# Attention of the next batch element in six large blocks instead of twelve, beside a Strassen-like channel mixing on one core

## The chip, the cores and the metric

The kernel runs on one NeuronCore of a Trainium2 chip. The metric is the device time of one execution in microseconds. The core has five engines that work side by side and wait for one another through semaphores: TensorE (PE, with its weight loads shown apart as PEld), VectorE (DVE), ScalarE (ACT), GpSimd (POOL) and SyncE (SP), which here only issues DMA transfers.

## The reference

Everything is float32: 8 batch elements, 12 heads, sequence 448, head size 64, so 768 channels.

```python
# attention, per element and head
q_n, k_n = rmsnorm(q, g_q), rmsnorm(k, g_k)
attn = softmax(q_n @ k_n.T / sqrt(64))
x = attn @ v                      # heads side by side: (448, 768) per element

# mixer, per element
h  = relu(x.T @ w_tok1) @ w_tok2  # token mixing, 448 -> 256 -> 448
u  = x + h.T
h2 = relu(u @ w_ch1) @ w_ch2      # channel mixing, 768 -> 1536 -> 768
out = u + h2
```

The mixer of an element needs the whole attention of that element, and nothing of any other element.

## The kernel before

**What runs when.** `whole` writes one long program. Its loop over `b` emits the mixing of element `b`, and, spread into it, the attention of element `b + 1` (`AHEAD = 1`). The last element's mixing (`b = 7`) therefore stands alone. In what follows "phase b" is one round of this loop. A phase is, on TensorE: `tok1` (L685) and `tok2` (L693) for the token mixing; then the channel mixing as block-wise products after Strassen and Winograd: `ch1` (L809) makes 21 products (3 column groups `mp` of 7 products `i`), `ch2` with group 0 (L866) makes 14 halves (7 products, `j` = 0 and 1, which share one PSUM tile), and `ch2` with group 1 makes 7 more at the end. Each of these 42 items is 6 matmuls of 128x128 weights with 224 columns; the trace shows every float32 matmul as two records. Element 0 is mixed with plain products (L781) while its weights are converted from 64-bit floats. This conversion (`convert_first`, L264 to L282) uses two small tiles from `cv_pool`.

**Product results.** Every `ch1` product goes to a PSUM tile `m_ps` from a pool of two (`ps_M`), and must be read out before the second product after it can start. By `i`, the reader is: 0 ScalarE (L818), 1, 2, 3 VectorE (L814), 4 ScalarE (L830, followed by two GpSimd additions), 5 and 6 VectorE. `put_off` keeps some work until the beginning of the next product, such as the two VectorE maxima L839 after product 5. `ch2` is alike (L875, L879).

**Attention.** Heads are handled in pairs, and pairs two at a time: `t` counts the pairs of pairs, three to an element. For each `t` there are seven key blocks `k`. `score(t, k)` is four 64x64 matmuls (L385), one in each quarter of TensorE, into two PSUM tiles of the pool `ps_S` (four tiles), then two exponentials on ScalarE (L389) into a tile `e`, of which there are four. `values` (L459) multiplies the exponentials with `v`. `group_sums` (L427) adds up the seven `e` tiles, the first two additions on GpSimd and the rest on VectorE; `row_sums` (L439) finishes the sum on TensorE; `denominators` (L488 to L505) inverts and scales on VectorE. `score`, `values` for one `k`, and `row_sums` are of the same size on TensorE; they are called units of attention here, 45 in a full phase.

**Preparing q and k** for the next `t`: `square` (ScalarE, L1173), `reduce` (VectorE, L1187), `roots`, which is `fold` (four ScalarE copies, L1195), `guess` (VectorE, L1204 and L1209) and three `newton` steps (nine small VectorE operations, L1228 to L1230); then `scale` (L350) and `turn_qk` (VectorE transposes L365, one ScalarE multiplication L368). `square` writes one shared tile `sq`, so the second pair's square waits for the first pair's reduce.

**The order.** On the four compute engines the order is the order in which the program is written (`manual_schedule`); each engine works its list strictly in turn. SP's list is ordered by the framework. `att_step(g)` makes the items of a quarter of one `t`: `tiled`, a block of 3 or 4 units of attention on TensorE, and around it the items for the other engines. There are 12 such steps in a phase. `merge` interleaves lists of items (cost, function) in proportion to their costs, so that the 12 steps are spread evenly over `tok1` with `h = 1`, `tok2`, `ch1` and most of `ch2`. The last 4 halves of `ch2` group 0 and group 1 (`last`) have no attention beside them.

**DMA.** Weights come back from a scratch area in units (L740), eight buffers ahead; `load_units` for a product waits until the buffer of an earlier product is free. Loads of q and k (L1154, 16 for each `t`), of `v` (L338), the attention result's way through DRAM (`send_x`, L639, and `load_x`, L646), and the output (L629) share the same SP queue.

Of the kernel before, what the change touches and what calls it, by code (L numbers as in the profile page):

```python
# [8 lines left out]
F32 = mybir.dt.float32  # L9
U32 = mybir.dt.uint32  # L10
# [34 lines left out]
def whole(ctx, tc, shifted, pre, q, k, v, g_q, g_k, moe_w_tok1, moe_w_tok2, moe_w_ch1, moe_w_ch2, out):  # L45


    nc = tc.nc
# [3 lines left out]
    B, H, S, D = q.shape  # L52
# [3 lines left out]
    P = 128  # L56
    NS = 4
    R = S // NS
    NPAIR = H // 2
    NP = B * NPAIR  # L60
# [5 lines left out]
    HS = S // 2  # L66
    KC, KF = NC // 2, NF // 2
# [3 lines left out]
    NK = S // D  # L71
    NB = S // 32
    assert S == NK * D and NPAIR % 2 == 0 and D % 32 == 0

    UNITS = 8

    pool = lambda name, bufs, **kw: ctx.enter_context(tc.tile_pool(name=name, bufs=bufs, **kw))
    const = pool("const", 1)
    raw_pool = pool("raw_pool", 5)
    cv_pool = pool("cv_pool", 2)  # L80
    pre.st_pool = pool("st_pool", 2)
    pre.nt_pool = pool("nt_pool", 2)
    qkT_pool = pool("qkT_pool", 3)
# [17 lines left out]
    w1_sb = const.tile([P, NS, DT], F32, name="w1_sb")  # L101
    w2_sb = const.tile([P, NJ, NS, R], F32, name="w2_sb")
    hb = pre.hb

    ws1 = dram.tile([KF // 2, NQ, P, KC, 2, P], F32, name="ws1")
    ws2 = dram.tile([2, NQ, P, 3, 2, P], F32, name="ws2")
# [2 lines left out]
    st = dict(pre.st)  # L109
# [18 lines left out]
                pending.pop(0)[1]()  # L128

    WCOLS = 512

    def weight_chunks():

# [121 lines left out]
    def convert_first(i):  # L257

        if chunks[i][1][0].dtype != I64:
            return  # L260
        rows, n = chunks[i][0], columns(i)
        lo, hi = (st["raw", i][0:rows, 0:n, w] for w in range(2))
        e = cv_pool.tile([P, WCOLS], U32, name="e_t")[0:rows, 0:n]
        nc.vector.tensor_scalar(e, hi, 0x000FFFFF, 0x00100000, ALU.bitwise_and, ALU.bitwise_or)  # L264
        nc.vector.scalar_tensor_tensor(  # L265
            out=lo.bitcast(F32), in0=lo, scalar=2.0**-32, in1=e, op0=ALU.mult, op1=ALU.add)
        nc.vector.tensor_scalar(e, hi, 0x7FF00000, None, ALU.bitwise_and)
        st["cv", i] = e
# [102 lines left out]
        if i == 0:  # L371
            st.pop(("qk", p))

    def e_tile():
        return e_pool.tile([P, 2, S], F32, name="e")

    def score(t, k):

        e = st["e", t, k] = e_tile()
        pss = [s_tile("s_ps") for i in range(2)]  # L380
        for i in range(2):
            qkT = st["qkT", 2 * t + i]
            for a in range(2):
                h = slice(a * D, a * D + D)
                nc.tensor.matmul(  # L385
                    out=pss[i][rows_of(i, a), 0:S], lhsT=qkT[h, 1, k * D:(k + 1) * D], rhs=qkT[h, 0, :],
                    start=True, stop=True)
        for i in range(2):
            nc.scalar.activation(out=e[:, i, :], in_=pss[i][:, 0:S], func=AF.Exp)  # L389
# [77 lines left out]
    def row_sums(t):  # L467
        es = st.pop(("es", t))
        for p in (2 * t, 2 * t + 1):
            st["d", p] = s_tile("d_ps")  # L470
            ones(p, es[:, p % 2, :], start=True, stop=True)
# [38 lines left out]
        return parts + [lambda p=p: end(p) for p in ps]  # L510

    NG = 2 * NP

    def att_step(g):


        t, s = divmod(g, 4)
        p = 2 * t
        pair = (p, p + 1)
        live = g < NG  # L520
        items = []

        def finish():
            if s == 0 and t:
                last = (p - 2, p - 1)
                for k in (NK - 2, NK - 1):
                    values(last, k)
            if live:
                for k in ((0,), (1, 2), (3, 4), (5, 6))[s]:
                    score(t, k)  # L530
            if s == 0 and t:
                if not on_pe(p - 1):
                    row_sums(t - 1)
                for i in last:
                    st.pop(("v", i))

        def tiled():
            if shifted:
                if live:
                    both_shifted()  # L540
            else:
                finish()
            if live and s == 3:
                for i in pair:
                    st.pop(("qkT", i))
            if inside:
                for fn in turns:
                    fn()
            if live and s and not shifted:
                for k in ((), (0,), (1, 2), (3, 4))[s]:  # L550
                    values(pair, k)

        def both_shifted():
            i = p + s // 2
            if s % 2 == 0:
                score_shifted(i)
                return
            for k in range(NK):
                values((i,), k)
            for k in range((NK + 1) // 2):  # L560
                st.pop(("e1", i, k))
            st.pop(("v", i))
            for part in denominators((i,)):
                part()

        n = p + 2
        ahead, behind, turns = [], [], []
        f = lambda fn, *pairs: [lambda i=i: fn(i, st) for i in pairs]  # L570
        scales = lambda n: [lambda i=i: scale(i) for i in (n, n + 1)]
        if g in (1, 5):
            ahead, behind = f(pre.square, g // 4 * 2 + 4), f(pre.reduce, g // 4 * 2 + 4)
        elif g in (2, 6):
            ahead, behind = f(pre.square, g // 4 * 2 + 5), f(pre.reduce, g // 4 * 2 + 5)
        elif g in (3, 7):
            behind = pre.roots(g // 4 * 2 + 4, st)
        elif g in (4, 8):
            behind = scales(g // 4 * 2 + 2)
        if live and n < NP:  # L580
            late = n < 2 * NPAIR + 2
            if t >= NPAIR // 2 and late:
                if s == 1:
                    ahead, behind = f(pre.square, n), f(pre.reduce, n) + f(pre.square, n + 1)
                elif s == 2:
                    behind = f(pre.reduce, n + 1) + pre.roots(n, st) + scales(n)
            elif t >= NPAIR // 2:
                a, b = f(pre.square, n) + f(pre.reduce, n), f(pre.square, n + 1) + f(pre.reduce, n + 1)
                behind = (a, b + pre.roots(n, st), scales(n), [])[s]
            now = {2: [] if pre.plain(n) else [n], 3: [n, n + 1] if pre.plain(n) else [n + 1]}.get(s, [])  # L590
            turns = [lambda q=q, i=i: turn_qk(q, i) for q in now for i in (1, 0)]

        inside = g < 2 * NPAIR
        items += [(0.3, fn) for fn in ahead]
        items.append((2.4 if s == 1 else 3.2, tiled))
        part = lambda fns, c=0.4: [(c, fn) for fn in fns]
        if s == 0 and t and not shifted:
            items += part(denominators((p - 2, p - 1)))
        if live and not on_pe(p):
            items += [(0.5, lambda k=k: group_sums(t, k)) for k in ((), (1, 2), (3, 4), (5, 6))[s]]  # L600

        if s == 0 and 5 < p + 1 < NP:
            items.append((0.0, lambda: load_v(p + 1)))
        if live and s == 1 and 5 < p + 2 < NP:
            items.append((0.0, lambda: load_v(p + 2)))
        js = []
        if live and s == 0:
            js = [n, n + 1] if pre.plain(p) else [n + 1]
        elif live and s == 3 and not pre.plain(n):
            js = [n + 2]  # L610
        items += [it for j in js if pre.first_slot + 2 <= j < NP
                  for it in part(pre.loads(j, st, nc.sync, nc.sync), 0.2 if pre.plain(j) else 0.6)]
        if g == 3:
            items += [it for j in (6, 7) for it in part(pre.loads(j, st, nc.sync, nc.sync), 0.2)]
        items += part(behind)
        if not inside:
            items += part(turns)
        return items


# [298 lines left out]
    us = lambda n, cols: n * cols * 4 / 2400  # L919

    def x_items(b, h):
        return [(0.1, lambda j=j: trans_x(b, j)) for j in range(h * NC // 2, (h + 1) * NC // 2)]
# [4 lines left out]
    def middle_items(b):  # L927

        items = []
        for t in range(KC):  # L930
            items += [(us(NJ, S), lambda cc=cc: tok2(b, cc)) for cc in (t, KC + t)]
            if b:
                items.append((0.0, lambda t=t: moving_sums(b, t)))
        if b == 0:
            return items, [(us(4, S), lambda n=n: first_stage(n)) for n in range(len(stages))]
        items += [(us(6, HS), lambda mp=mp, i=i: ch1(b, mp, i)) for mp in range(KF // 2) for i in range(7)]
        return items, [(us(6, HS), lambda i=i, j=j: ch2(b, 0, i, j)) for i in range(7) for j in range(2)]

    def in_next(b):

# [38 lines left out]
    AHEAD = 1  # L979
# [33 lines left out]
    scale(2)  # L1013
    scale(3)
    per = NPAIR * 2
    att_items = lambda lo, hi: [it for g in range(lo, hi) for it in att_step(g)]

    run(merge(
        att_items(0, 8) + merge(att_items(8, AHEAD * per + 1), x_items(0, 0)), weight_items(0, BEFORE)))
    left, (some, direct, sums) = [], sum_items()  # L1020
    for b in range(B):
# [15 lines left out]
            early, last = early[:-4], early[-4:]  # L1037
        lo = (b + AHEAD) * per + 1
        att = []
        if b + AHEAD < B:  # L1040
            att = att_items(lo, lo + 10) + x_items(b + AHEAD, 0) + att_items(lo + 10, lo + per)
        if b == 0:
            last = x_items(1, 1) + merge(last, direct + sums[:5], turns(b, y_order(b)[2:4]))
        else:
# [260 lines left out]
```

## Time and profile before

| | us |
|---|---|
| median of 3 runs (1344.58 to 1347.64) | 1346.51 |
| span of the profiled execution | 1343.4 |
| PE busy with matmuls | 1284.4 |
| VectorE, ScalarE, GpSimd busy | 757.2, 368.7, 385.1 |
| phase 1 (mixing element 1, from its first L685 to the next phase's) | 162.73 |
| phases 2 to 5, each | 157.6 |
| phase 6 | 152.79 |
| phase 7, without attention (PE busy) | 114.95 |
| 12 records of a channel product | 2.27 |

The span is the time of one profiled execution between its first and last instruction; the runs also hold what lies around it. The table of seven phases comes from asking the trace for windows that begin where `tok1` begins: L685 starts at 272.66, 435.39, 593.0, 750.58, 908.17, 1065.75 and 1218.54 us. Busy time of PE is the union of its matmuls, and weight loads (PEld) overlap with them. A gap in PE that the trace marks with a releaser is a wait; a gap marked "issue" is one that no semaphore explains. The chain of work that ended last runs mostly over PE:

```profile
PE 72%; DVE 15%; DMA 4%; POOL 3%; issue 2%; ACT 2%; SPq 1%; DVEq 0%; ACTq 0%; POOLq 0%
```

### The profile page before, as it was taken

The numbers are of one execution on the slowest core, as the hardware profiler recorded it, in microseconds if no ns is written. First come the engines' busy times: TensorE is split into PE (matmuls) and PEld (weight loads), VectorE is DVE, ScalarE is ACT, GpSimd is POOL, SyncE is SP. The second block draws the span as 40 slices with busy tenths as digits, with TensorE's granted clock in tenths as the row PEclk, the third lists the DMA queues.
The fourth block names the chain that finished last, engine by engine and source line by source line (L and its number), as shares of the span: only waits on it lengthen the run. The fifth ranks groups of instructions, "written<-read, shape, count | busy, mean of one in ns | idle before, by whom it ended". The sixth has DMA issues, their size and how long they took to land.

```text
span 1343.4 us, 20171 instructions
## 1 busy us (share of the span) xinstructions
PE 1284.4 (96%) x7408; PEld 926.5 (69%) x7408; DVE 757.2 (56%) x1289; ACT 368.7 (27%) x740; POOL 385.1 (29%) x449
## 2 busy tenths in 40 slices
PE   5989998989999999999999999999999999999997
PEld 3344444447779477885779667794777867787996
DVE  6887689646764555626664365645556365543212
ACT  5553433123230333212331223302332033300100
POOL 1211540356561223211331222312332033211220
PEclk9999999889999999999999999999999999999998
DMA  9665488889889556794549665594666955476554
GB/s 207 167 170 152 128 221 204 189 234 235 230 204 253 118 154 161 157 223 107 144 117 230 145 153 147 123 254 96 158 158 151 232 119 151 125 189 139 176 172 92
DMA packets 501520, 227.82 MB, mean 170 GB/s; under 512 B 373604, under 2 KB 463076, under 8 KB 501412
## 3 DMA queue, kind: packets, MB, share of 16 engines
q1 hardware_dynamic: 488290, 224.60, 67.9%
q10 hardware_dynamic: 12994, 1.84, 0.8%
q8 instruction: 61, 1.00, 0.3%
q14 instruction: 47, 0.39, 0.1%
q0 software_dynamic: 128, 0.00, 0.0%
HBM read 186.84 MB, written 39.52 MB: 169 GB/s over the span
## 4 chain that ended last, share of the span: by engine, by line
PE 72%; DVE 15%; DMA 4%; POOL 3%; issue 2%; ACT 2%; SPq 1%; DVEq 0%; ACTq 0%; POOLq 0%
PE m_ps L866 25%; PE m_ps L809 19%; PE o_ps L459 7%; PE s_ps L385 7%; PE m_ps L685 5%; PE m_ps L693 4%; DVE es L427 2%; DVE qk_t L350 2%; DMA raw<-in_moe_w_ch_dram 1%; DVE raw L265 1%; DVE raw L282 1%; PE m_ps L781 1%; PE d_ps L439 1%; ACT e L389 1%; DMA unit<-ws 1%
## 5 line engine op out<-in xcount | busy, mean ns | idle before, releaser
L866 PEld LDWEIGHTS m_ps<-hb,unit 128*128 128x128 f32 x1764 | 332.1, 190 | 13.7 <-issue 10.2
L866 PE MATMUL m_ps<-hb,unit 128*128 128x224 f32 x1764 | 339.5, 354 | 0.0
L809 PE MATMUL m_ps<-tu,unit 128*128 128x224 f32 x1008 | 202.6, 355 | 3.8 <-DVE r L814 3.8
L809 PEld LDWEIGHTS m_ps<-tu,unit 128*128 128x128 f32 x1008 | 188.4, 190 | 21.8 <-DVE r L814 7.0
L389 ACT ACTIVATE e<-s_ps 128x448 f32<-128x448 f32 x336 | 157.0, 547 | 99.0 <-PE s_ps L385 98.0
L809 PE MATMUL m_ps<-uT,unit 128*128 128x224 f32 x756 | 154.6, 357 | 6.1 <-ACT r L830 2.5
L385 PE MATMUL s_ps<-qkT 64*64 64x448 f32 x1260 | 147.9, 551 | 9.0 <-ACT qkT L368 4.8
L809 PEld LDWEIGHTS m_ps<-uT,unit 128*128 128x128 f32 x756 | 140.6, 190 | 22.8 <-DVE uT L698 5.7
L459 PE MATMUL o_ps<-e,v 64*64 64x448 f32 x1316 | 150.9, 544 | 0.1
L875 POOL TENSOR_TENSOR uT<-uT,r 128x448 f32<-128x448 f32 (+1 forms) x56 | 52.8, 954 | 263.7 <-DVE r L875 148.9
L814 DVE TENSOR_TENSOR r<-m_ps,r 128x448 f32<-128x448 f32 x63 | 39.0, 619 | 122.5 <-PE m_ps L809 68.3
L875 DVE TENSOR_TENSOR uT<-uT,m_ps 128x448 f32<-128x448 f32 (+1 forms) x70 | 34.1, 503 | 124.5 <-PE m_ps L866 124.5
L427 DVE TENSOR_TENSOR es<-es,e 128x896 f32<-128x896 f32 x84 | 92.6, 1102 | 15.5 <-ACT e L389 12.5
L459 PEld LDWEIGHTS o_ps<-e,v 64*64 64x64 f32 x1316 | 50.9, 134 | 70.6 <-issue 64.6
L385 PEld LDWEIGHTS s_ps<-qkT 64*64 64x64 f32 x1260 | 44.5, 132 | 79.5 <-issue 60.2
L814 POOL TENSOR_TENSOR hb<-r,r 128x448 f32<-128x448 f32 x21 | 27.9, 1327 | 236.0 <-ACT r L830 186.7
L693 PE MATMUL m_ps<-w_sb,h 128*128 128x448 f32 x192 | 80.6, 564 | 7.7 <-DVE uT L698 7.7
L685 PE MATMUL m_ps<-x,w_sb 112*128 112x384 f32 x256 | 86.4, 490 | 1.3 <-ACT x L665 1.0
L368 ACT ACTIVATE qkT<-qkT,g_t 128x448 f32<-128x448 f32 x36 | 24.1, 668 | 214.8 <-DVE qkT L365 214.8
L427 POOL TENSOR_TENSOR es<-e 128x896 f32<-128x896 f32 x21 | 44.1, 2101 | 131.8 <-ACT e L389 131.8
L685 PEld LDWEIGHTS m_ps<-x,w_sb 112*128 112x128 f32 x256 | 47.8, 190 | 37.7 <-ACT e L389 4.2
L1187 DVE TENSOR_REDUCE ms<-sq 128x28 f32<-128x896 f32 (+2 forms) x45 | 48.7, 1084 | 44.4 <-ACT sq L1173 41.8
(117 smaller groups left out, 1378.7 us busy)
## 6 DMA issues: line engine op xcount, KB each, us to landing
unit<-ws SPq DMA_DIRECT2D x294, 384.0 KB, 4.2
raw<-in_moe_w_ch_dram SPq DMA_DIRECT2D x72, 256.0 KB, 3.7
v<-in_v_dram SPq DMA_DIRECT2D x94, 112.0 KB, 4.4
xs<-xt SPq DMA_DIRECT2D x56, 168.0 KB, 4.5
x<-xs SPq DMA_DIRECT2D x14, 672.0 KB, 6.7
out_dram<-turned SPq DMA_DIRECT2D x168, 56.0 KB, 2.0
qk_t<-in_q_dram SPq DMA_DIRECT2D x144, 56.0 KB, 2.7
qk_t<-in_k_dram SPq DMA_DIRECT2D x144, 56.0 KB, 3.7
```

Source lines behind the costliest of these rows:

```text
L350: nc.vector.tensor_tensor(out=x, in0=x, in1=r.unsqueeze(2).to_broadcast(list(x.shape)), op=ALU.mult)
L385: nc.tensor.matmul(out=pss[i][rows_of(i, a), 0:S], lhsT=qkT[h, 1, k * D:(k + 1) * D], rhs=qkT[h, 0, :], start=True, stop=True)
L389: nc.scalar.activation(out=e[:, i, :], in_=pss[i][:, 0:S], func=AF.Exp)
L427: eng.tensor_tensor(out=es[:], in0=(es if k > 1 else st["e", t, 0])[:], in1=st["e", t, k][:], op=ALU.add)
L459: nc.tensor.matmul(out=st["o", p][a * D:(a + 1) * D, 0:S], lhsT=vt[rows, k * D:(k + 1) * D], rhs=e[rows, :], **kw)
L685: nc.tensor.matmul(out=ps[:, 0:HC], lhsT=w1_sb[0:R, c, jc * P:(jc + 1) * P], rhs=st["x", b, h][0:R, :, c, :], start=(c == 0), stop=(c == N ...
L693: nc.tensor.matmul(out=ps[:, 0:S], lhsT=st["h1", jc][:, cc * P:(cc + 1) * P], rhs=w2_sb[:, jc].rearrange("p c r -> p (c r)"), start=(jc == ...
L809: nc.tensor.matmul(out=ps[:, j * HS:(j + 1) * HS], lhsT=w[:, t, j, :], rhs=m, start=(t == 0), stop=(t == KC - 1))
L814: add = lambda e, o, x, y: e.tensor_tensor(out=o, in0=x, in1=y, op=ALU.add)
L866: nc.tensor.matmul(out=ps[:, j * HS:(j + 1) * HS], lhsT=st["w"](j, t), rhs=hb[:, HB[what], t, :], start=(t == 0), stop=(t == KF - 1))
L875: add = lambda e, o, x, y: e.tensor_tensor(out=o, in0=x, in1=y, op=ALU.add)
L1187: self.nc.vector.tensor_reduce(out=st["ms", p][:, p % 2, lo:hi], in_=sq[:, lo:hi], axis=AX_X, op=ALU.add)
```

## The change

From phase 1 on (the attention of elements 2 to 7) the twelve steps become six blocks, two to each `t`, written by `big_step`. The first block of a `t` holds scores 0 and 1, the values 4, 5, 6 of the `t` before, the row sums of that `t`, and score 2: 7 units. The second holds scores 3 and 4, values 0 to 3, scores 5 and 6: 8 units. Each block comes with four lists: `ahead` (before the last item ahead of the block), the block, `beside` (written directly behind the block: for a first block the second reduce and the roots; for a second block scale, turns and two group sums) and `between` (spread by `place` over the mixing items up to the next block: denominators, loads, the other turns and group sums).

`place` puts the blocks at fixed mixing items. `BLOCKS = (0, 6, 11, 17, 22, 28)` counts the 35 `ch1` and `ch2` group 0 items, and a block stands in front of its item: second blocks at 0, 11 and 22, first blocks at 6, 17 and 28. `tok1` and `tok2` have no attention between them any more. The step that ended phase 0 is replaced by the first big block of element 2, with two scores that phase 1 held before.

The two conversion tiles become one fixed tile `cv_sb`; from element 2 on, when conversion is over, every fifth `e` tile lives in it, so that five are in rotation.

```diff
+    WCOLS = 512
-    cv_pool = pool("cv_pool", 2)
+    cv_sb = const.tile([P, 2, WCOLS], F32, name="cv_sb")
...
-        e = cv_pool.tile([P, WCOLS], U32, name="e_t")[0:rows, 0:n]
+        e = cv_sb[0:rows, i % 2, 0:n].bitcast(U32)
...
-    def e_tile():
+    def e_tile(spare=False):
+
+        if spare:
+            return cv_sb[:].rearrange("p i n -> p (i n)")[:, 0:2 * S].rearrange("p (i s) -> p i s", i=2)
         return e_pool.tile([P, 2, S], F32, name="e")
 
     def score(t, k):
 
-        e = st["e", t, k] = e_tile()
+        e = st["e", t, k] = e_tile(t >= BIG and ((t - BIG) * NK + k) % 5 == 4)
...
+    BIG = NPAIR
+
+    def big_step(t, second):
+
+        p, n = 2 * t, 2 * t + 2
+        pair, last, live, more = (p, p + 1), (p - 2, p - 1), p < NP, 2 * t + 2 < NP
+        item = lambda fn, *a, c=0.4: (c, lambda: fn(*a))
+        loads = lambda j: [(0.3, fn) for fn in pre.loads(j, st, nc.sync, nc.sync)] if j < NP else []
+
+        def first_block():
+            if live:
+                score(t, 0)
+                score(t, 1)
+            if more:
+                pre.reduce(n, st)
+                pre.square(n + 1, st)
+            for k in range(NK - 2 - (t > BIG), NK):
+                values(last, k)
+            row_sums(t - 1)
+            for i in last:
+                st.pop(("v", i))
+            if live:
+                score(t, 2)
+
+        def second_block():
+            score(t, 3)
+            score(t, 4)
+            for k in range(4):
+                values(pair, k)
+            score(t, 5)
+            score(t, 6)
+            for i in pair:
+                st.pop(("qkT", i))
+
+        if not second:
+            ahead = [item(pre.square, n, st)] if more else []
+            beside = [item(pre.reduce, n + 1, st)] + [(0.4, fn) for fn in pre.roots(n, st)] if more else []
+            between = [(0.4, fn) for fn in denominators(last)]
+            between += [item(load_v, i, c=0.0) for i in pair if live]
+            between += [item(group_sums, t, k) for k in (1, 2) if live]
+            return ahead, (5.4, first_block), beside, between
+        beside = [item(scale, n), item(scale, n + 1), item(turn_qk, n, 1), item(turn_qk, n, 0)] if more else []
+        beside += [item(group_sums, t, k) for k in (3, 4)]
+        between = [item(turn_qk, n + 1, 1), item(turn_qk, n + 1, 0)] + loads(n + 2) if more else []
+        between += [item(group_sums, t, k) for k in (5, 6)] + loads(n + 3)
+        return [], (6.2, second_block), beside, between
+
+    def place(units, blocks, at):
+
+        res, i, rest = [], 0, []
+        for j, (ahead, block, beside, between) in list(zip(at, blocks)) + [(len(units), ([], None, [], []))]:
+            n, done = j - i, 0
+            for m in range(n):
+                if m == n - 1 and block:
+                    res += ahead
+                res.append(units[i + m])
+                upto = -(-len(rest) * (m + 1) // n)
+                res += rest[done:upto]
+                done = upto
+            if not n:
+                res += rest + ahead
+            i, rest = j, between
+            if block:
+                res += [block] + beside
+        return res
...
+        if g == 4 * BIG - 1 and not shifted:
+            items += part(pre.loads(n + 3, st, nc.sync, nc.sync), 0.3)
...
+    BLOCKS = (0, 6, 11, 17, 22, 28)
...
-        if b + AHEAD < B:
-            att = att_items(lo, lo + 10) + x_items(b + AHEAD, 0) + att_items(lo + 10, lo + per)
+        if b + AHEAD < B and (shifted or not b):
+            att = att_items(lo, lo + 10) + x_items(b + AHEAD, 0) + att_items(lo + 10, lo + per - (b == 0 and not shifted))
+            if not shifted:
+                ahead, block, beside, between = big_step(BIG, False)
+                att += ahead + [block] + beside + between
+        elif b + AHEAD < B:
+            t = (b + AHEAD) * NPAIR // 2
+            blocks = [big_step(t + i // 2, i % 2) for i in range(1, NPAIR + 1)]
+            blocks[4][3].extend(x_items(b + 1, 0))
+            early = place(early, blocks, [near(early, at) for at in BLOCKS])
```

`near(early, at)` returns the place of the `at`-th of these 35 items in the list. The branch named `shifted` serves inputs with larger scores; it is not taken here and stays as it was.

More of the change, by code (lines that the diff above doesn't have):

```diff
@@ L128, in run @@
                 pending.pop(0)[1]()
-    WCOLS = 512
     def weight_chunks():
@@ L936, in middle_items @@
         items += [(us(6, HS), lambda mp=mp, i=i: ch1(b, mp, i)) for mp in range(KF // 2) for i in range(7)]
-        return items, [(us(6, HS), lambda i=i, j=j: ch2(b, 0, i, j)) for i in range(7) for j in range(2)]
+        double = [(us(6, HS), lambda i=i, j=j: ch2(b, 0, i, j)) for i in range(7) for j in range(2)]
+        mixing.update(fn for _, fn in items[3 * KC:] + double)
+        return items, double
     def in_next(b):
@@ L1015, in whole, with near @@
     per = NPAIR * 2
+    BLOCKS = (0, 6, 11, 17, 22, 28)
+    def near(units, at):
+        seen = [i for i, (c, fn) in enumerate(units) if fn in mixing]
+        return seen[at]
+    mixing = set()
     att_items = lambda lo, hi: [it for g in range(lo, hi) for it in att_step(g)]
```

## The prediction

> **What bounds the kernel now.** First the page's busy table, then the seven mixing phases as windows, cut where tok1 (L685) starts. Columns there: length, then busy time and instructions of PE, PEld, DVE, ACT and POOL, granted clock, DMA share, GB/s.
>
> ```profile
> PE 1284.4 (96%) x7408; PEld 926.5 (69%) x7408; DVE 757.2 (56%) x1289; ACT 368.7 (27%) x740; POOL 385.1 (29%) x449
> ```
> ```profile
> 272.66:435.39 162.73, 156.68 (x921) 118.34 (x920) 93.86 (x151) 42.37 (x88) 85.72 (x122) 0.98 0.92 234
> ...
> 750.58:908.17 157.59, 154.73 (x922) 117.39 (x921) 85.67 (x152) 41.76 (x87) 39.77 (x32) 1.00 0.66 159
> ...
> 1065.75:1218.54 152.79, 152.40 (x913) 117.19 (x913) 77.79 (x132) 36.16 (x76) 40.40 (x32) 1.00 0.62 154
> 1218.54:1343.40 124.86, 114.95 (x561) 105.71 (x560) 30.99 (x56) 11.23 (x21) 25.55 (x26) 0.97 0.52 137
> ```
>
> TensorE is the bound. The last phase has no attention and shows what mixing alone costs it: 114.95 us. A middle phase takes 157.58 with 45 attention units. (A unit is one score block, or one value block of two pairs, or the row sums: 8 records in two groups of four concurrent ones, 0.375 us a group, so 0.75 us.) 157.58 - 114.95 - 33.75 = 8.9 us are neither. Two things make it up. The timeline of PE gives the stalls (start, length, then idle before and its releaser); the same five recur in phases 2 to 5:
>
> ```profile
> 777.18 3.36 PE L693 MATMUL m_ps<-w_sb,h 128*128 128x448 f32 x8 [0.95 <-DVE uT L698]
> ...
> 783.25 2.54 PE L809 MATMUL m_ps<-uT,unit 128*128 128x224 f32 x12 [0.34 <-DVE uT L698]
> ...
> 797.18 2.54 PE L809 MATMUL m_ps<-uT,unit 128*128 128x224 f32 x12 [0.62 <-ACT r L830]
> ...
> 827.40 2.54 PE L809 MATMUL m_ps<-uT,unit 128*128 128x224 f32 x12 [0.18 <-DVE r L814]
> ...
> 840.88 2.54 PE L809 MATMUL m_ps<-tu,unit 128*128 128x224 f32 x12 [0.76 <-DVE r L814]
> ```
>
> Sum 2.85. The timeline of the weight loads gives the rest, the price of entering and leaving a block of 64x64 matmuls:
>
> ```profile
> 804.25 4.54 PEld L809 LDWEIGHTS m_ps<-uT,unit 128*128 128x128 f32 x24
> 809.07 0.21 PEld L385 LDWEIGHTS s_ps<-qkT 64*64 64x64 f32 x8 [0.28 <-issue]
> ...
> 811.38 0.15 PEld L459 LDWEIGHTS o_ps<-e,v 64*64 64x64 f32 x4 [0.22 <-issue]
> 812.24 0.86 PEld L809 LDWEIGHTS m_ps<-tu,unit 128*128 128x128 f32 x5 [0.70 <-ACT e L389]
> ```
>
> The next load was due at 804.25 + 4.54 = 808.79 and came at 812.24: 3.45 us for eight groups of 0.375 = 3.00, so 0.45 lost. Inside the block, from scores to values, the spacing stays 0.375. Twelve blocks a phase make 5.4; 5.4 + 2.85 = 8.25 of the 8.9.
>
> Phase 1 has one stall that costs twice (PE timeline, then a window):
>
> ```profile
> 296.53 5.88 PE L693 MATMUL m_ps<-w_sb,h 128*128 128x448 f32 x8 [3.90 <-DVE uT L698]
> ```
> ```profile
> 296.00:303.00 7.00, 6.47 (x16) 2.88 (x20) 6.12 (x9) 0.00 (x0) 3.62 (x4) 0.58 0.83 178
> ```
>
> The idle stretch is followed by 5.8 us at about half clock, another 2.9 us.
>
> [...] a 1.62 us idle at 224.61 left the clock at 1.00. [...] in phase 1 the chain from L1204 to L1230 took 7.0 us (288.96 to 295.95) beside a busy GpSimd, and 2.9 us where GpSimd was free.
>
> **The change part by part.** Big blocks serve phases 1 to 6; the units and their number stay.
>
> (a) Fewer switches. 72 blocks become 36: 36 x 0.45 = -16.2 us. Nothing hides these now, as PE is the bound, so all of it counts.
>
> (b) Stalls that go. tok1 and tok2 no longer have attention between them, so VectorE's L698 isn't behind L427 and L350, and tok2's last evictions lie under the first block. Denominators no longer stand before the eviction that PE waits for at 840.88; ScalarE's product copies no longer stand behind exps. Phases 2 to 5: 4 x 2.87 = 11.5; phase 1: 3.90 + 2.9 + 1.13 + 0.76 = 8.7; phase 6: 0.4. Together -20.6. The last phase shows tok1, tok2 and products without attention and without such a gap.
>
> (c) A stall that comes. In a first block ScalarE's order is exps of scores 0 and 1, a square, exps of score 2, and then the four fold copies; score 2 is the block's last PE work. VectorE's order behind the block is L1204 (needs the folds), the guess, nine Newton operations, and only then the next product's eviction.
>
> ```profile
> 806.29 1.00 ACT L1195 COPY half<-ms 32x56 f32<-32x56 f32 x4 [2.88 <-DVE ms L1187]
> ...
> 807.33 0.46 DVE L1204 SCALAR_TENSOR_TENSOR ms<-ms,half 128x56 f32<-128x56 f32 x1 [1.07 <-ACT half L1195]
> ...
> 831.42 0.93 PE L385 MATMUL s_ps<-qkT 64*64 64x448 f32 x8
> ...
> 832.48 0.98 ACT L389 ACTIVATE e<-s_ps 128x448 f32<-128x448 f32 x2 [0.73 <-PE s_ps L385]
> ```
> ```profile
> 764.90 0.19 DVE L1209 TENSOR_SCALAR rs<-ms 128x56 int32<-128x56 int32 x1
> ...
> 767.26 0.61 DVE L698 TENSOR_TENSOR uT<-uT,m_ps 128x448 f32<-128x448 f32 x1
> ```
>
> From the start of score 2 (zero): exps end at 832.48 + 0.98 - 831.42 = 2.04; folds at 3.1; L1204 0.49; guess and Newton 767.26 - 764.90 = 2.36; VectorE is free at 5.95. PE starts the next product at 0.86 (the value of the block at 832) and takes 2.264 for each (168 records in 31.70 us). Its two m_ps buffers let two products run, to 5.39; the third needs the first one's eviction.
> - Block at product 6: that eviction stands behind the two maxima of L839 (1.15) as well and ends at 5.95 + 1.15 + 0.6 = 7.7: stall 2.3.
> - At product 17: 5.95 + 0.6: stall 1.2.
> - At product 28 the buffer holds two products and is wanted at 7.65: none.
> Six and five of these have roots to compute (phase 6 has no pair left for its second): 6 x 2.3 + 5 x 1.2 = +19.8. The denominators behind them end about when the next buffer is due: +1 for all. In phase 1 GpSimd is busy 85.72 us against 40 and would hold VectorE's small operations. Bounds: nothing, to the whole 7.0 - 2.9 = 4.1 on both stalls with 2.9 of half clock on each, 14. I take +4, since GpSimd's L427 pieces, which did the holding at 289 to 293, now come after the Newton steps.
>
> (d) Hidden parts. Second blocks last 6 us on PE and carry 2.0 + 1.2 + 2.2 us of L350, L365 and L427 on VectorE, which PE doesn't need before its second product. Exps: score 5 comes 4.5 us after score 3, whose exps end 2.04 after it, so PSUM is free; the e rotation keeps five tiles (cv_sb as the fifth), and each has its last reader before the scores that need it. SP: q and k loads (16 a pair of pairs, some 0.5 us each to issue) gather in the 13.6 us behind second blocks. By the order on SP the last three stand behind a weight load that waits for the fourth product, so they go out some 2.5 us before the first block and land (3.7 us median) 1 to 2 us into it; their square is due at 3.2 and does harm only after 4.6. The x load for tok1's second half had at least 5 us to spare over its 6.7 us landing; the missing block there takes 2.4 of it. Nothing is charged.
>
> Sum: -16.2 - 20.6 + 19.8 + 1 + 4 = -12.0. Against the profiled 1343.4 us of span that is 1331.4; the runs lie about 3.1 above the span (1346.5 median), so 1334.5.
>
> **The rivals.**
> - B, no new stall: if the folds come before the last exps in effect, or evictions aren't held, (c) falls away: 1334.5 - 24.8 = 1309.7. For it: VectorE is 44% idle. Against: both orders in (c) are strict.
> - C, no gain: [...] the gains are re-spent on new stalls of the same size: 1346.5. [...]
> - D, slower. The place is the same hold, in front of the roots. If q and k loads land late, or the Newton chain is held by e more, every first block pays e, and [...] half clock adds 2.9 each. At e = 1.5: 6 x 4.4 + 5 x 1.5 + 5 x 0.45 = 36: 1370. It decides from e = 1.1, where it is worth over 12 us even without the clock. For it: the 7.0 us chain in phase 1 and the DMA share, which reaches 1.00 in crowded stretches. Against: from phase 2 GpSimd has no work queued beside the roots, and the loads have about 3 us of slack.
>
> **How the numbers follow.** A (forecast) 0.57, own range 1323 to 1345 (from 0 to 14 in phase 1, stalls off by half a us each); B 0.11; C 0.08; D 0.24. The range 1309 to 1354 takes in A, B, C and the near end of D. About 0.2%, 2.7 us, is what a measurement tells from no change. Faster: A, B and a little of C, 0.69; same 0.06; slower 0.25.
>
> **What would show it.** (a): middle phases near 155 us with six blocks, 0.45 at each. (b): no idle before L693. (c): PE idle of about 2.3 us before the third product after the block at 6, 1.2 after the one at 17, released by the eviction, with the Newton operations directly before it on VectorE and folds behind exps on ScalarE. [...] squares waiting for qk_t loads inside first blocks, would mean D; no idle there, B. Blocks that cost more than 0.45, or gaps inside them at exps or PSUM, would make the sum wrong altogether.

## The result, and the profile after

| us | before | after |
|---|---|---|
| median of 20 runs each | 1346.53 (1343.57 to 1349.19) | 1347.88 (1343.38 to 1354.87) |
| span of the profiled execution | 1343.4 | 1347.5 |
| ahead of the first `tok1` | 84.95 | 86.1 |
| phase 0 | 187.7 | 195.9 |
| phase 1 | 162.7 | 175.2 |
| phase 2 | 157.6 | 154.0 |
| phases 3 to 5, each | 157.6 | 153.6 |
| phase 6 | 152.8 | 150.5 |
| phase 7 | 124.9 | 124.9 |

The ratio is 1.001, interval 0.9998 to 1.0022: no change that can be measured, where 1334.5 was forecast. The table says more than the total. Its phases are of one profiled execution of each kernel; these two lie 4.1 us apart in span, the medians 1.4, and the executions of the kernel after spread over 11.5 us (before: 5.6). Phases 2 to 6 gained 17.7 us, twice the forecast for them. Phases 0 and 1 lost 8.2 and 12.5. Two attention units (1.5 us) have moved from phase 6 to phase 0 with the new block there: phase 0 has 765 PE records against 748, phase 6 has 898 against 913. So 1.5 of the 8.2, and 1.5 of phase 6's gain of 2.3, is only work counted elsewhere. Two questions follow: why the middle did better, and what happens in the first two phases. The page's busy table hides both; PE is even busy for 8 us less:

```profile
PE 1276.4 (95%) x7408; PEld 937.7 (70%) x7408; DVE 748.0 (56%) x1289; ACT 370.5 (27%) x740; POOL 383.1 (28%) x449
```

In the table of windows of the kernel after (columns as before: length, busy time and records of PE, PEld, DVE, ACT, POOL, clock, DMA share, GB/s), these are phases 0, 1 and 4:

```profile
86.10:282.04 195.94, 182.24 (x765) 86.04 (x766) 150.48 (x236) 66.49 (x126) 62.50 (x92) 0.96 0.65 166
282.04:457.20 175.16, 158.85 (x921) 123.07 (x920) 86.42 (x151) 42.53 (x88) 82.23 (x122) 0.94 0.87 222
...
764.84:918.49 153.65, 151.30 (x922) 118.29 (x921) 86.25 (x152) 42.17 (x87) 40.62 (x32) 1.00 0.68 162
```

Phase 4 has 2.35 us of PE idle left; phase 1 has 16.3, and a granted clock of 0.94. The timeline of PE in phase 4 shows both idles (start, length, then idle before and its releaser). They are the forecast's new stalls, at the blocks in front of products 6 and 17:

```profile
816.30 2.54 PE L878 MATMUL m_ps<-uT,unit 128*128 128x224 f32 x12 [1.69 <-DVE hb L883]
...
854.18 2.54 PE L878 MATMUL m_ps<-uT,unit 128*128 128x224 f32 x12 [0.65 <-DVE r L883]
```

The same view over phases 0 and 1 shows what was not forecast:

```profile
208.13 8.16 PE L850 MATMUL m_ps<-hb,stage 128*128 128x448 f32 x13 [4.61 <-ACT hb L862]
...
250.96 2.19 PE L441 MATMUL d_ps<-es,one_c 64*64 64x448 f32 x8 [4.83 <-ACT e L391]
...
290.54 8.19 PE L754 MATMUL m_ps<-x,w_sb 112*128 112x384 f32 x16 [3.18 <-DMA x<-xs]
...
349.72 4.73 PE L878 MATMUL m_ps<-uT,unit 128*128 128x224 f32 x12 [10.19 <-DVE hb L883]
...
391.22 4.22 PE L878 MATMUL m_ps<-uT,unit 128*128 128x224 f32 x12 [2.08 <-DVE r L883]
```

The lengths are as telling as the idles: twelve records of a product take 4.73 and 4.22 us here, 2.54 elsewhere, so these waits cost some 2 us more behind them, at a lower clock (0.64 and 0.59 in windows behind the last two). Phase 1 adds up: without its old stalls and switches it would be a phase of about 151.3 us (an estimate: 162.7 less the forecast's 2.7 and 8.7). Idles of 3.18, 0.86 (at 332.52), 10.19 and 2.08 make 16.3, and the slow records behind them 2.9 (8.19, clock 0.65, against 5.33 for the 16 records from 282.04, clock 1.00), 2.2 and 1.7: 174.4 of 175.2.

The 10.19 us is the same chain as the 1.69 of phase 4, started late. The timeline of all engines ahead of it (SPq is SP's DMA queue):

```profile
334.11 0.39 SPq L240 DMA_DIRECT2D raw<-ws  x1
334.60 0.45 SPq L211 DMA_DIRECT2D ws<-raw  x1
...
336.43 2.31 SPq L1241 DMA_DIRECT2D qk_t<-in_k_dram  x2
...
342.24 0.95 ACT L1260 ACTIVATE sq<-qk_t 128x896 f32<-128x896 f32 x1 [8.47 <-DMA ws<-raw]
...
345.37 0.22 DVE L1291 SCALAR_TENSOR_TENSOR ms<-ms,half 128x56 f32<-128x56 f32 x1 [1.07 <-ACT half L1282]
...
347.98 1.15 DVE L908 SCALAR_TENSOR_TENSOR hb<-r,hb 128x448 f32<-128x448 f32 x2
...
349.05 0.61 DVE L883 TENSOR_TENSOR hb<-m_ps,r 128x448 f32<-128x448 f32 x1
```

The block begins at 327.67. The second pair's square in it needs k loads that SP issued from 336.43, 8.8 us into the block, between reads and writes of the weight sums (`raw<-ws`, `ws<-raw`). The square's named releaser is one of those neighbours; it reads `qk_t`, so the load is the likelier cause, which the runs below test. Everything else follows at the steady pace: reduce and folds to 345.34, 2.7 us from L1291 to the last Newton step, two maxima, the eviction, PE.

The 4.61 in phase 0 reads alike: the eviction L862 stands on ScalarE behind a square that waited 5.94 us for the first pair's reduce, and that stands on VectorE behind a weight conversion whose load came 2.93 us late. The 4.83 is the new block itself, whose exps stand behind a square that waited 4.84 for its load. The timeline of all engines:

```profile
199.27 2.08 POOL L429 TENSOR_TENSOR es<-e 128x896 f32<-128x896 f32 x1 [16.84 <-ACT e L391]
199.64 1.99 DVE L263 TENSOR_SCALAR cv_sb<-raw 128x512 uint32<-128x512 uint32 x1 [2.93 <-DMA raw<-in_moe_w_ch_dram]
...
206.60 0.95 ACT L1260 ACTIVATE sq<-qk_t 128x896 f32<-128x896 f32 x1 [5.94 <-DVE ms L1274]
...
248.30 0.95 ACT L1260 ACTIVATE sq<-qk_t 128x896 f32<-128x896 f32 x1 [4.84 <-DMA qk_t<-in_q_dram]
```

The late load isn't all of the 4.61. Two operations of the conversion, L263 and L264, took 1.99 and 2.45 us there, beside two group sums of GpSimd; a few us later, where no sum runs, they take 0.43 and 0.69. That is 3.3 us more in the same chain.

In the page's chain of waits VectorE's share is 3%, against 15% before. The shares add up to 80% here and to 99% before, so this view can't say where the rest is; the phases can.

```profile
PE 69%; DVE 3%; DMA 3%; ACT 2%; POOL 1%; SPq 1%; issue 1%; ACTq 0%; DVEq 0%; POOLq 0%
```

### The profile page after: what moved, and what is told of

Its sections match the earlier page's. It is cut to its first block, busy times and chain, and to the rows that moved or that the text cites. A ratio compares the mean times of both kernels' runs of the same rounds, so it can differ in the third digit from the quotient of the medians.

```text
span 1347.5 us, 20173 instructions
## 1 busy us (share of the span) xinstructions
PE 1276.4 (95%) x7408; PEld 937.7 (70%) x7408; DVE 748.0 (56%) x1289; ACT 370.5 (27%) x740; POOL 383.1 (28%) x449
## 4 chain that ended last, share of the span: by engine, by line
PE 69%; DVE 3%; DMA 3%; ACT 2%; POOL 1%; SPq 1%; issue 1%; ACTq 0%; DVEq 0%; POOLq 0%
PE m_ps L935 25%; PE m_ps L878 20%; PE s_ps L387 7%; PE o_ps L461 7%; PE m_ps L754 5%; PE m_ps L762 5%; PE d_ps L441 1%; ACT half L1282 1%; DMA qk_t<-in_k_dram 1%; DVE nt L1316 1%; DVE nt L1315 1%; DVE rs L1317 1%; DVE hb L908 0%; DMA ws<-raw 0%; ACT e L391 0%
## 5 line engine op out<-in xcount | busy, mean ns | idle before, releaser
L391 ACT ACTIVATE e<-s_ps 128x448 f32<-128x448 f32 x286 | 134.5, 549 | 213.5 <-PE s_ps L387 213.5
L878 PEld LDWEIGHTS m_ps<-uT,unit 128*128 128x128 f32 x756 | 144.6, 194 | 32.8 <-DVE hb L883 21.2
L461 PE MATMUL o_ps<-e,v 64*64 64x448 f32 x1116 | 129.2, 545 | 0.1
L944 POOL TENSOR_TENSOR uT<-uT,r 128x448 f32<-128x448 f32 (+1 forms) x56 | 49.6, 896 | 236.6 <-DVE r L944 151.1
L429 DVE TENSOR_TENSOR es<-es,e 128x896 f32<-128x896 f32 x70 | 83.3, 1190 | 21.1 <-POOL es L429 16.5
L883 POOL TENSOR_TENSOR hb<-r,r 128x448 f32<-128x448 f32 x21 | 23.8, 1133 | 245.7 <-ACT r L899 236.6
L461 PEld LDWEIGHTS o_ps<-e,v 64*64 64x64 f32 x1116 | 45.6, 135 | 62.3 <-issue 59.0
L1274 DVE TENSOR_REDUCE ms<-sq 128x28 f32<-128x896 f32 (+2 forms) x45 | 48.7, 1083 | 52.6 <-ACT sq L1260 50.0
L884 ACT ACTIVATE hb<-hb 128x448 f32<-128x448 f32 x63 | 36.3, 577 | 148.8 <-DVE hb L883 128.2
L762 PE MATMUL m_ps<-w_sb,h 128*128 128x448 f32 x192 | 74.7, 543 | 0.0
L767 DVE TENSOR_TENSOR uT<-uT,m_ps 128x448 f32<-128x448 f32 x48 | 29.4, 614 | 65.3 <-PE m_ps L762 65.3
```

The source lines that it names most:

```text
L429: eng.tensor_tensor(out=es[:], in0=(es if k > 1 else st["e", t, 0])[:], in1=st["e", t, k][:], op=ALU.add)
L461: nc.tensor.matmul(out=st["o", p][a * D:(a + 1) * D, 0:S], lhsT=vt[rows, k * D:(k + 1) * D], rhs=e[rows, :], **kw)
L762: nc.tensor.matmul(out=ps[:, 0:S], lhsT=st["h1", jc][:, cc * P:(cc + 1) * P], rhs=w2_sb[:, jc].rearrange("p c r -> p (c r)"), start=(jc == ...
L878: nc.tensor.matmul(out=ps[:, j * HS:(j + 1) * HS], lhsT=w[:, t, j, :], rhs=m, start=(t == 0), stop=(t == KC - 1))
L883: add = lambda e, o, x, y: e.tensor_tensor(out=o, in0=x, in1=y, op=ALU.add)
L884: relu = lambda x: nc.scalar.activation(out=x, in_=x, func=AF.Relu)
```

## The experiments

Theory 1 is that the steady phases gained and that the start lost it again: late q and k loads in phase 1, and the seam at the end of phase 0, where the first large block stands among the conversion of weights. The main rival is that large blocks as such are dear, so that the loss goes wherever they begin. Other variants price one term of the sum each. Times are medians; ratios are to runs of the kernel before on the same chip. The phases are of one profiled execution each, which need not be a median one: the one of "a phase later" is the slowest of six (1343.9), the one of "loads in one piece" among the fastest of ten (1338.1, of 1337.6 to 1347.3).

| variant | us | ratio (95%) | phase 0 | phase 1 | phase 4 |
|---|---|---|---|---|---|
| after | 1347.9 | 1.001 (0.9998 to 1.0022) | 195.9 | 175.2 | 153.6 |
| large blocks a phase later | 1339.0 | 0.994 (0.9925 to 0.9955) | 188.5 | 174.5 | 153.6 |
| loads in one piece | 1342.5 | 0.9964 (0.9947 to 0.9982) | 195.7 | 164.9 | 153.7 |
| fold ahead of score 2 | 1340.5 | 0.9946 (0.9929 to 0.9963) | 198.9 | 174.8 | 151.1 |
| blocks at 7 and 18 | 1395.1 | 1.0348 (1.0327 to 1.0369) | 196.8 | 189.5 | 160.2 |
| phase 0 as before | 1338.3 | 0.9933 (0.992 to 0.9947) | 187.6 | 171.0 | 153.7 |
| second blocks cut in two | 1358.0 | 1.0081 (1.0065 to 1.0096) | 197.1 | 177.5 | 154.7 |
| fold and loads | 1327.9 | 0.9861 (0.9845 to 0.9876) | 197.4 | 162.4 | 151.0 |
| fold, loads and phase 0 as before | 1317.3 | 0.9767 (0.9744 to 0.9789) | 188.7 | 163.2 | 151.1 |
| blocks at 7 and 18, and fold | 1369.9 | 1.0162 (1.013 to 1.0195) | 197.4 | 182.4 | 155.3 |

### Large blocks a phase later

```diff
-    BIG = NPAIR
+    BIG = NPAIR // 2 * 3
...
-        if b + AHEAD < B and (shifted or not b):
+        if b + AHEAD < B and (shifted or b < 2):
...
```

> Twelve small steps in phase 1 as before; the first big block stands at the end of phase 1, and big blocks serve phases 2 to 6. Theory 1 (the gain is real in phases 2 to 6, 3.9 us in each of 2 to 5 and 2.3 in phase 6, and was lost in phases 0 and 1, where the loads of q and k come late beside the weight work): phase 0 is back at 272.7, phase 1 near 162, phases 2 to 5 stay near 153.7, the time falls to about 1329. Theory 2 (starting with big blocks costs some 20 us wherever the start is): phases 1 and 2 lose together what phases 0 and 1 lost, and the time stays near 1347.

Phase 0 came back to 188.5, as theory 1 has it (the 272.7 in the expectation is the moment at which phase 0 ended before, not its length). But phase 1, now with twelve small steps and with the two moved units, stayed at 174.5 in this execution, and the median lies half way between the two forecasts. The first large block now ends phase 1, and its square waits for loads there. The timeline of ScalarE:

```profile
416.15 0.95 ACT L1260 ACTIVATE sq<-qk_t 128x896 f32<-128x896 f32 x1 [12.59 <-DMA qk_t<-in_q_dram]
```

The row sums of that block waited 8.76 us for exps behind this square. Phase 1 also has its old stall ahead of `tok2`, 4.58 us here. So the rival is half right: the first block brings a loss with it. It is a seam's loss, though, not one of large blocks: phases 3 to 5 take 153.6 or 153.7 with this edit and without.

### The loads of a block in one piece

All 16 loads of q and k are written directly behind the turns of the second block, instead of spread over the products up to the next one.

```diff
-        between = [item(turn_qk, n + 1, 1), item(turn_qk, n + 1, 0)] + loads(n + 2) if more else []
-        between += [item(group_sums, t, k) for k in (5, 6)] + loads(n + 3)
+        def all_loads():
+            for _, fn in loads(n + 2) + loads(n + 3):
+                fn()
+        between = [item(turn_qk, n + 1, 1), item(turn_qk, n + 1, 0), (0.3, all_loads)] if more else []
+        between += [item(group_sums, t, k) for k in (5, 6)]
```

> All 16 loads of q and k stand directly behind the turns that free their buffers, instead of being spread to the next block. Theory 1 (phase 1 loses because the last k loads reach the queue behind weight traffic and the second square waits for them): the 10.2 us idle and its 2.3 us of half clock shrink to 3 us or less, phase 1 falls from 175 to about 163, later phases keep 153.7, the time is about 1336. Theory 2 (phase 1's transfers are short of bandwidth whatever their order, or weights come late now): phase 1 stays at 170 or more, and the time near 1347 or above.

Phase 1 got 10.3 us shorter in the profiled execution; phases 0 and 2 to 6 stayed within 0.4. The timeline of the same block, which begins at 326.50 here:

```profile
327.95 2.04 SPq L1244 DMA_DIRECT2D qk_t<-in_k_dram  x4
...
333.01 0.95 ACT L1263 ACTIVATE sq<-qk_t 128x896 f32<-128x896 f32 x1 [2.71 <-DMA qk_t<-in_k_dram]
...
340.51 3.73 PE L881 MATMUL m_ps<-uT,unit 128*128 128x224 f32 x9 [3.78 <-DVE hb L886]
```

The last load is issued up to 329.99, 3.5 us into the block instead of 11, the square starts 6.5 into it instead of 14.6, and PE's idle falls from 10.19 to 3.78. Only the place of the loads in the order changed. That the late loads made this stall is shown. The median fell by 5.4 us and not by the 12 expected; where the longer of the ten executions lose time isn't known, as none of them was profiled.

### The fold ahead of score 2

The second reduce and the four fold copies come before score 2, so that ScalarE has the folds in front of the last exps.

```diff
+            if more:
+                pre.reduce(n + 1, st)
+                pre.fold(n, st)
             if live:
                 score(t, 2)
...
-            beside = [item(pre.reduce, n + 1, st)] + [(0.4, fn) for fn in pre.roots(n, st)] if more else []
+            beside = [(0.4, fn) for fn in pre.roots(n, st)[1:]] if more else []
```

> In first blocks the second reduce and the fold copies stand before score 2 and its exps, so that the roots no longer wait for the block's last exps. Theory 1 (the 1.7 and 0.65 us before the third product are the roots held by those exps): both idles go, phases 2 to 5 fall from 153.7 to about 151.3, phase 6 by 1.7, and the time to about 1337; the 10 us idle of phase 1, which waits for a late square, stays. Theory 2 (the eviction is late for another reason, such as GpSimd's hold of VectorE): idles and time stay as in the changed kernel.

Phases 3 to 5 are 151.1, and the idles of 1.7 and 0.65 are gone. The timelines show the two orders exchanged on ScalarE, first phase 4 of the kernel after, then phase 3 of this run:

```profile
809.90 0.98 ACT L391 ACTIVATE e<-s_ps 128x448 f32<-128x448 f32 x2 [1.83 <-PE s_ps L387]
810.90 1.00 ACT L1282 COPY half<-ms 32x56 f32<-32x56 f32 x4
```
```profile
656.56 0.99 ACT L1285 COPY half<-ms 32x56 f32<-32x56 f32 x4 [1.15 <-DVE ms L1277]
...
657.57 0.98 ACT L391 ACTIVATE e<-s_ps 128x448 f32<-128x448 f32 x2
```

In the first one the second reduce (L1274) had ended at 809.20, so the folds had their input while ScalarE stood idle up to 809.90; they came behind the exps all the same, in the order of the program. So the mechanism of step (c) is right, and 2.6 us a phase (153.65 to 151.06) is its whole price. The stall of 9.92 us in phase 1 remained, as it must if loads make it. Two things got worse that weren't forecast: the idle at phase 1's next first block grew from 2.08 to 4.05, and phase 0 became 3.0 us longer. So the median gained 7.4 us instead of 11.

### First blocks one product later

```diff
-    BLOCKS = (0, 6, 11, 17, 22, 28)
+    BLOCKS = (0, 7, 11, 18, 22, 28)
```

> First blocks stand before products 7 and 18 instead of 6 and 17; second blocks stay. Both next products are then read out by ScalarE, so that the third product behind the block doesn't wait for VectorE behind the roots, and the fourth has one product more of time. Theory 1 (the idle is the eviction behind the roots): no idle at either, phases 2 to 5 at about 151.3, the time about 1337. Theory 2 (the idle comes with the roots wherever they are): idles of 1.7 and 0.65 stay, one product later, and so does the time.

This forecast failed by far: idles of about 4.57 and 1.61 in each of phases 2 to 5, which take 159.2 to 160.3 us. Phase 1 grew too, by 14.3; that was not read. The Newton operations of one chain, beside GpSimd, in the timeline:

```profile
522.78 0.22 DVE L1315 SCALAR_TENSOR_TENSOR nt<-rs 128x56 f32<-128x56 f32 x1
...
524.09 2.08 POOL L429 TENSOR_TENSOR es<-e,cv_sb 128x896 f32<-128x896 f32 x1
524.24 2.00 DVE L1317 SCALAR_TENSOR_TENSOR rs<-nt,rs 128x56 f32<-128x56 f32 x1
...
531.80 2.45 PE L878 MATMUL m_ps<-tu,unit 128*128 128x224 f32 x7 [4.58 <-DVE hb L883]
```

An operation of 0.22 us takes 2.00 while a group sum runs on GpSimd. In the kernel after, with the block at 6, this doesn't happen: GpSimd's next operation, L910, waits for the maxima L908, and they stand behind the chain on VectorE. With the block one product later the maxima come first, and GpSimd's work starts 0.7 us after the chain. Three operations of the chain are held so and take 5.30 us together instead of 0.66. The edit has a second effect: the four operations of the denominators up to 531.27 now stand ahead of the eviction that PE waits for, 1.6 us; with the block at 6 they stand behind it. The places chosen by the change are worth 6.6 us a phase through both, and no run here takes them apart.

> Blocks at products 0, 7, 11, 18, 22 and 28 as in the run that moved them, and with it the fold of the early roots ahead of score 2. Theory 1 (the moved blocks lost time because the Newton chain came to stand beside GpSimd's two group sums, which slowed its small VectorE operations from 0.22 us to about 2): with the fold ahead the chain starts about 2 us earlier and is done before them, so that the idle of 4.57 us at the first block falls under 1.5 and the steady phases go from 160.2 to 152 or 153; total near 1343. Theory 2 (the place itself is bad: the chain meets GpSimd's work wherever in that block it starts, or the eviction waits for something else): the idle stays above 3 us, phases 157 to 160, total 1375 to 1395. A mean VectorE time of 0.22 us for the half's product decides for theory 1, one above 1 us for theory 2.

With the fold ahead as well (the two edits above together) the result lies between both theories: idle 2.90 instead of 4.57, phases of 155.3 to 156.9. The chain now starts 1.7 us ahead of GpSimd instead of 0.7, enough for five of its nine Newton operations; the sixth meets it:

```profile
516.35 0.22 DVE L1319 TENSOR_TENSOR nt<-nt,ms 128x56 f32<-128x56 f32 x1
516.57 1.13 POOL L920 TENSOR_TENSOR hb<-hb 128x448 f32<-128x448 f32 x1 [6.27 <-issue]
516.60 1.18 DVE L1320 SCALAR_TENSOR_TENSOR rs<-nt,rs 128x56 f32<-128x56 f32 x1
```

Until GpSimd starts each operation takes 0.22, from then on 1.18, 2.01 and 2.12, and the ninth, when the sums are over, 0.22 again. That is the hold itself, within one chain. It cost 4.65 us, as much as without the fold (4.64); the idle fell by the 1.67 us by which the chain begins earlier after score 2 (1.34 instead of 3.01), and by no more. Theory 1 named a true cause and was wrong on the size. The sign that it named, the time of the half's product, could not decide: that operation took 0.22 in both runs.

### Phase 0 as before

Phase 0 keeps its twelve small steps, with its old loads; one small step of the next element, which phase 1 needs to have, goes into phase 1's beginning.

```diff
-            for k in range(4):
+            for k in range(t == BIG, 4):
                 values(pair, k)
...
-        if g == 4 * BIG - 1 and not shifted:
-            items += part(pre.loads(n + 3, st, nc.sync, nc.sync), 0.3)
...
+                if not shifted:
+                    begin = merge(begin, att_items(4 * BIG + 1, 4 * BIG + 2))
...
-            att = att_items(lo, lo + 10) + x_items(b + AHEAD, 0) + att_items(lo + 10, lo + per - (b == 0 and not shifted))
-            if not shifted:
-                ahead, block, beside, between = big_step(BIG, False)
-                att += ahead + [block] + beside + between
+            att = att_items(lo, lo + 10) + x_items(b + AHEAD, 0) + att_items(lo + 10, lo + per)
```

> Only the start of the big blocks is changed: phase 0 keeps its twelve small steps to the end, phase 1 keeps one small step (scores 1 and 2, value 0) between its token mixing items, and the first big block is the second block of that pair of pairs. Theory 1 (phase 0 lost 8 us because the big block at its end needs squares whose loads come just before it): phase 0 returns to about 188 us, phase 1 stays at 170 to 176 because of its late k loads, phases 2 to 6 as in the changed kernel; the time falls by about 8 to 1339. Theory 2 (phase 0 lost through something else in the program, such as the fixed conversion tile): phase 0 stays near 196 and the time near 1347.

Phase 0 is 187.6, as in the kernel before, and phase 1 became 4.1 shorter, although the two moved units now stand in it (937 PE records against 921). The wait for `x` at the start of phase 1 is gone with the block at the end of phase 0: the load of `x` goes out 0.5 us ahead of the first `tok1`, in the kernel after 2.7 us behind it. Against that stand two new waits of 1.28 and 2.36 us for a weight sum of GpSimd (`tu`). The idle at product 6 stayed, 9.68 us. So seam and loads are two separate losses. Which of the two parts, the block or the eight loads that the change added for it, hurts phase 0 more was not tried apart.

### Second blocks cut in two

Scores 5 and 6 stand one product later than the rest of the block: three more switches a phase, the same work.

```diff
+        def second_rest():
             score(t, 5)
             score(t, 6)
...
+        if second == 2:
+            return [], (1.5, second_rest), [], []
...
+        between = [(0.0, lambda: None)] * 5 + between
...
+            for i in (0, 2, 4):
+                rest = big_step(t + (i + 1) // 2, 2)
+                at = near(early, BLOCKS[i] + 1)
+                rests.append((at, rest[1]))
+            early = place(early, blocks, [near(early, at) for at in BLOCKS], rests)
```

> Each second block is cut in two: scores 5 and 6 stand one product later. Nothing else moves by more than a fraction of a product. Theory 1 (0.45 us for every change of tile mode and back): three more blocks a phase cost 1.35 us, phases 2 to 5 rise from 153.7 to about 155.0, the time by 8. Theory 2 (the gain of phases 2 to 6 came from the stalls removed, not from fewer switches): phases stay at 153.7.

Phase 4 rose by 1.09 us, from 153.65 to 154.74, with the idles at 1.70 and 0.67 as before: 0.36 a switch, under the 0.45 of step (a). Phases 0 and 1 moved too, by 1.2 and 2.3, so the total says less than the phases.

### The parts together

> Loads behind the turns, and fold and second reduce before score 2, together. Theory 1 (two separate causes): the gains add, phase 1 about 164, phases 2 to 5 at 151.1, phase 6 at 149, phase 0 still 196, the time about 1332. Theory 2 (both relieve the same wait): about 1339.

Fold and loads together: 1327.9, better than expected, with 162.4 in phase 1 and 151.0 in phase 4. The two gains do more than add: the medians fell by 7.4 and 5.4 us alone and by 20.0 together. The idle of 4.05 that the fold alone left in phase 1 is gone.

> The start of seam with the loads and the fold of lf. Theory 1: phase 0 at 188, phase 1 about 163, phases 2 to 5 at 151.1, phase 6 at 149: the time is about 1322. Theory 2 (the 8 us of phase 0 move into phase 1 with the start): about 1331.

With phase 0 as before in addition the kernel takes 1317.3 us (1310.24 to 1319.25), 2.3% less than the kernel before, and does the same work. Its phases, by windows:

```profile
86.16:274.82 188.66, 177.92 (x748) 84.33 (x749) 147.38 (x224) 63.83 (x117) 58.84 (x90) 0.96 0.68 174
274.82:438.00 163.18, 157.34 (x937) 121.71 (x936) 91.41 (x163) 46.56 (x97) 87.84 (x124) 0.98 0.89 235
589.20:740.30 151.10, 151.07 (x922) 118.49 (x921) 85.34 (x152) 42.28 (x87) 40.89 (x32) 1.00 0.67 165
```

In the last row PE's idle is 0.03 us. The three repairs together gave 7.3 in phase 0, 11.9 in phase 1 and 12.4 in phases 2 to 6. Phase 1 still takes 12 us more than a steady phase. 1.5 of that is the two moved units; the trace shows two waits of 2.36 and 2.35 us for a weight sum on GpSimd and a clock of 0.79 around them. That was not followed further.

## Why the prediction was wrong

- **(a) 36 fewer switches, -16.2: right, a little too large.** A steady phase without idle takes 151.1 us; mixing and attention units make 114.95 + 33.75 = 148.7. That leaves 2.4 for six blocks, 0.40 each; the cut blocks gave 0.36. At these prices the term is 13 to 14.4.
- **(b) Stalls that go, -20.6: right.** None of them is left in phases 2 to 6, nor in phase 1. In phases 2 to 5 the two terms together were worth more than the sum had: 157.6 - 151.1 = 6.5 us a phase against 2.7 + 2.87, about 1 us more. The forecast's account of a phase had left 0.65 unexplained. What the rest is stays open.
- **(c) The new stall: right mechanism, too large in the steady phases.** At the places forecast, with the chain forecast, 1.69 and 0.65 instead of 2.3 and 1.2. L1204 (L1291 after) took 0.22, not the 0.49 taken from before. The eviction ended 7.3 us after the start of score 2, not 7.7, and PE's two free products reached to 5.67, not 5.39. Phases 2 to 6 came out 9.4 us better than forecast (-17.7 against -8.3): 4.8 is this stall, 0.8 the denominators' +1, which did not show, 1.5 the two units that moved to phase 0, and the rest, 2.3, lies in (a) and (b).
- **(c) in phase 1, +4, bounds 0 to 14: the named cause was not the one.** GpSimd did not hold the chain: its operations took 0.22 us. The chain was late.
- **(d) "Nothing is charged": this step failed.** It placed the loads "some 2.5 us before the first block" in every phase alike, and left a slack of about 3 us. In phases 3 to 5 that holds; in phase 2 a square already waits 1.90 us for its load. In phase 1 SP's list also carries the weight sums' traffic, and the loads went out up to 11 us into the block: phase 1 took 175.2 where the sum had 159.0, 16.2 more. Of this the loads in one piece gave back 10.3. The large block at the end of phase 0, with its own loads among the weight conversion, was not priced at all. Phase 0 took 8.2 us more; 1.5 of them are the moved units, and 6.7 are loss. With phase 0 as before they were gone, and so was the wait for `x` behind that block, which (d) had judged to have 5 us to spare.

The account closes: 1331.4 of span forecast, -9.4 in phases 2 to 6, +16.2 in phase 1, +8.2 in phase 0, +1.1 ahead of the first `tok1`: 1347.5, as in the profile. The last term means little, as that stretch takes 85.0 to 88.3 us in the eleven profiles. That the total came out almost where it was before is a coincidence of these terms. Of the rivals, D had the mechanism that decided ("If q and k loads land late"), but spread it over every first block; it happened at one block and at the seam. The hold by GpSimd, which D also names, lengthened the 4.61 in phase 0 and none of the chains behind first blocks that PE waited for in phases 1 to 6.

## What to carry to other kernels

A slack that is measured in steady phases says nothing of the phase that still shares the queue with other work. For every transfer that a change moves, read its queue in the most crowded phase, and price the first and the last instance of a pattern on their own. And a total that hasn't moved may hide two large terms: cut the trace into phases before judging a mechanism.

## What the runs showed of the hardware

- **Waits of nearly the same length were followed by different clocks.** In the kernel after, 2.05 us of idle ahead of 509.02 left twelve records at 2.54 us (clock 1.00), but 2.08 ahead of 391.22 was followed by twelve in 4.22 (clock 0.59), and 2.90 in the run with moved blocks and fold by twelve in 3.64 (clock 0.68). No run here shows what makes the difference, nor from which idle on the clock falls; the 2.9 us that rival D adds at product 6 are an estimate from the one stall of 3.90 us in phase 1 before. The measurement decides: of these idles of 2 to 3 us two cost another 1.1 and 1.7 us, and one cost nothing.
- **Beside one GpSimd operation of 2.08 us a VectorE operation of 0.22 took 2.00**; in the run with moved blocks the nine Newton operations, 0.22 each when free, had means of 0.44 to 0.52. A conversion with a single input tile (L263), 0.43 when free, took 1.99 in phase 0 beside a group sum of 2.08.
